# Attention and MLP on one core: four token groups' second layer as seven half-size products, and the attention output kept in a ring

## The chip, the cores and the metric

The kernel runs on one NeuronCore of a Trainium2 chip. The core's engines are TensorE (PE, matrix products into the accumulator memory PSUM), VectorE (DVE), ScalarE (ACT), GpSimd (POOL) and SyncE (SP, which here only issues transfers). Each takes its own instructions in order; semaphores order them among each other. The metric is the device time of one execution in microseconds (us), the median over runs.

## The reference, cut to what matters

The program computes attention with 16 extra "beacon" keys in front of 576 causal ones, for 8 batches and 8 heads of depth 64, and then a two-layer MLP with a gate over all 4608 tokens.

```python
k_all = np.concatenate([beacon_k, k], axis=2)          # 8, 8, 592, 64
scores = scale * np.matmul(q, k_all.transpose(0, 1, 3, 2))
scores = np.where(causal, -1000000000.0, scores)
a = softmax(scores)                                    # over the keys
x = (a @ v_all)  ->  4608 tokens x 512
h = x @ w_in                                           # 512 x 2048
g = h * (1.0 / (1.0 + np.exp(-1.702 * h)))
out = g @ w_out                                        # 2048 x 512, float32
```

## The kernel before, in words

All matrix products have f16 inputs and accumulate in float32.

**Attention.** Work is cut into 16 sets `s`: 8 batches times two half-sets of four heads. For a set, `e_turn` transposes q and k on DVE (line 353), `e_qk` makes scores in chunks of up to 512 columns for four heads (line 382), `e_exp` exponentiates them on ACT (line 393) and `e_mask` clears what is not causal, on POOL (line 414; on DVE for two sets). `e_zadd` adds the exponentials of the key blocks on DVE (line 445: f16, both inputs in SBUF, six additions per set from the fifth set on). `e_av` multiplies by the values (line 467) and `e_norm` writes the normalised result, transposed, to the tile `xT` (line 496), which holds 512 features by all 4608 tokens.

**MLP.** Tokens are taken in ten groups: two of 256 and eight of 512 (`GROUPS`). `e_m1` makes one chunk of the first layer in one PSUM bank: 128 hidden features by 512 tokens as four matmuls of 512 columns (line 518), or, in the groups of 256 tokens, two times 128 features by 256 tokens as eight matmuls of 256 columns. `e_tanh` (ACT, line 532) and `e_gate` (DVE, line 539) turn a chunk into the gated activations, in the group's tile `g` (128 partitions, 16 blocks of hidden features, 512 tokens). A chunk's bank is free again when its gate has read it. `e_m2` is the second layer: for each tile `mt` of 128 tokens it adds up 16 matmuls of 512 columns (line 551), planned in four quarters. `e_evac` copies the result times 0.5 to SBUF on ACT (line 565), `e_store` sends it out from SP (line 571).

**Order.** Nothing is scheduled at run time. The class `Plan` holds every step with an engine, an assumed duration, its dependencies, a priority and a due time, and lays all steps out in one order per engine; the program is emitted in that order. PE steps that need a PSUM bank of the `psu` pool take one of a ring of four (`RING`), the one that is free first. Attention chunks get due times spaced evenly from `T_ATT0` to `T_ATT1`; between them `choose` fills PE with first and second layer steps, in turn if both are ready. The assumed durations only shape the order.

Of the kernel before, what the change touches and what calls it, by code (L numbers as in the profile page):

```python
# [162 lines left out]
def kernel(  # L163
# [37 lines left out]
    ep = ctx.enter_context(tc.tile_pool(name="ep", bufs=NE))  # L201
    zp = ctx.enter_context(tc.tile_pool(name="zp", bufs=2))
    gp = ctx.enter_context(tc.tile_pool(name="gp", bufs=2))
    sp = ctx.enter_context(tc.tile_pool(name="sp", bufs=3))
    pss = ctx.enter_context(tc.tile_pool(name="pss", bufs=1, space=bass.MemoryType.PSUM))
    psu = ctx.enter_context(tc.tile_pool(name="psu", bufs=1, space=bass.MemoryType.PSUM))
# [2 lines left out]
    ones = cst.tile([P, 32], F16, tag="ones", name="ones")  # L209
    w1t = cst.tile([P, NKT, DFF], F16, tag="w1", name="w1")  # L210
    w2t = cst.tile([P, NNT, DMODEL], F16, tag="w2", name="w2")
    xT = cst.tile([P, NKT, NTOK], F16, tag="xT", name="xT")
    bkf = cst.tile([P, NSET, D], F32, tag="bkf", name="bkf")
    bkn = cst.tile([P, 2, D], F16, tag="bkn", name="bkn")
    qn = [cst.tile([P, TR * D], F16, tag=f"qn{i}", name=f"qn{i}") for i in range(NB3)]
# [276 lines left out]

    def e_norm(s, x, half):
        b, hs = divmod(s, HS)
        t0 = b * S + half * HF
        nc.vector.tensor_tensor(  # L496
            out=xT[:, 2 * hs + x, t0 : t0 + HF],
            in0=rings[("av", s, x, half)][:, 0:HF],
            in1=zs[(s, half)][1][:, :],
            op=ALU.mult,  # L500
        )
# [7 lines left out]
    def e_m1(g, n0, n1):  # L509
        t0, t1 = GROUPS[g]  # L510
        w = t1 - t0
        if n0 == 0:
            gts[g] = gp.tile([P, NNT, 512], F16, tag="g", name="g")
        u = ring_tile(("m1", g, n0))
        for nt in range(n0, n1):
            o = (nt - n0) * w
            for kp in range(NKT):
                nc.tensor.matmul(  # L518
                    u[:, o : o + w],
                    w1t[:, kp, nt * P : (nt + 1) * P],  # L520
                    xT[:, kp, t0:t1],
                    start=(kp == 0),
                    stop=(kp == NKT - 1),
                )

    sigs = {}

# [30 lines left out]

    osbs = {}

    def e_evac(g, mt, eng):
        osb = sp.tile([P, DMODEL], F32, tag="osb", name="osb")
        osbs[(g, mt)] = osb
        if eng == "ACT":
            nc.scalar.mul(out=osb[:, :], in_=rings[("m2", g, mt)][:, :], mul=0.5)  # L565
        else:
            nc.vector.tensor_scalar_mul(osb[:, :], rings[("m2", g, mt)][:, :], 0.5)

    def e_store(g, mt):
        t0 = GROUPS[g][0] + mt * P  # L570
        nc.sync.dma_start(out=out[t0 : t0 + P, :], in_=osbs[(g, mt)][:, :])


    T_ATT0, T_ATT1 = 11000, 245000
    NCH0 = 4 * HS
    T_CH = (T_ATT1 - T_ATT0) / (len(CHUNKS) - NCH0)

# [12 lines left out]
        return flight[-1]  # L590

    op = plan.op
    turn, qks, exps, masks, avs, norms = {}, {}, {}, {}, {}, {}
    vload = {}
    gates, m2s = {}, {}
# [83 lines left out]
    def values(s):  # L679
        b, hs = divmod(s, HS)  # L680
        whole = s >= ZSUM
        order = [(2, 1), (2, 0), (0, 0), (1, 0), (0, 1), (1, 1)] if whole else [
            (x, h) for h in range(2) for x in (2, 0, 1)
        ]
        sums, z2 = [], {}
        if whole:
# [16 lines left out]
        for n, (x, half) in enumerate(order):  # L703
            deps = after(s, 0, ETOT) if whole else after(s, half * EHALF, ETOT if half else EHALF)
            if x < 2:
                deps += [vload[(b, j)] for (j, _, _) in AVP[half]] + [vload[(b, -1)]]
# [55 lines left out]
    for j in range(-1, NJ):  # L762
        load_v(1, j)

    def mlp(g):
        t0, t1 = GROUPS[g]
# [7 lines left out]
        old = [m2s[(g - 2, mt, 3)] for mt in range((GROUPS[g - 2][1] - GROUPS[g - 2][0]) // P)] if g > 1 else []  # L774
        n = 512 // w
        for n0 in range(0, NNT, n):
            n1 = n0 + n
            key = ("m1", g, n0)
            pe = op(
                "PE", 4 * n * (w / 2.4 + 2.5), xs + w1_of[n0] + old, lambda n0=n0, n1=n1: e_m1(g, n0, n1),  # L780
                kind="m1", pr=g, ring=key, mode="m", name=f"m1.{g}.{n0}",
            )
            a = op("ACT", 555, [pe], lambda n0=n0, n1=n1: e_tanh(g, n0, n1), pr=1, name="tanh")
            gates[(g, n0)] = op(
                "DVE", 610, [a], lambda n0=n0, n1=n1: e_gate(g, n0, n1), pr=2, closes=key, name="gate"
            )
        for mt in range(w // P):
# [9 lines left out]
            ev = op("ACT", 560, [prev], lambda g=g, mt=mt: e_evac(g, mt, "ACT"), pr=1, closes=key, name="evac")  # L797
            op("SP", 60, [ev], lambda g=g, mt=mt: e_store(g, mt), name="store")

    g = 0  # L800
    for i, ch in enumerate(CHUNKS):
# [11 lines left out]
        for s, c0, c1 in ch:  # L813
            if c1 == ETOT:
                values(s)
                while s % HS == HS - 1 and g < NG and GROUPS[g][1] <= (s // HS + 1) * S:
                    mlp(g)
                    g += 1
    order = plan.run()
    for o in order:  # L820
        o.emit()
# [29 lines left out]
```

## Time and profile before

| | us |
|---|---|
| median of 3 runs | 344.96 (344.85 to 344.98) |
| the profiled execution | 345.13 |
| its span, first to last instruction | 343.4 |
| PE busy in it | 324.2 (94%) |
| DVE busy | 234.3 (68%) |
| ACT busy | 203.6 (59%) |
| POOL busy | 117.2 (34%) |

The granted TensorE clock is full in every one of the page's 40 slices. Line 551, the second layer, has 576 matmuls of 512 columns, 142.5 us busy in the page's list of groups; line 518, the first layer, has 512 of 512 columns and 128 of 256. A matmul's listed duration (379 ns for 512 columns) overlaps with the next one's, so its price in a stream is the spacing of starts. In the timeline attention's last additions over keys run at 248 us, and from then on only the last values and MLP work are left; the last first-layer chunk starts at 324.92 us.

### The profile page before, as it was taken

The numbers are of one execution on the slowest core, as the hardware profiler recorded it, in microseconds if no ns is written. First come the engines' busy times: TensorE is split into PE (matmuls) and PEld (weight loads), VectorE is DVE, ScalarE is ACT, GpSimd is POOL, SyncE is SP. The second block draws the span as 40 slices with busy tenths as digits, with TensorE's granted clock in tenths as the row PEclk, the third lists the DMA queues.
The fourth block names the chain that finished last, engine by engine and source line by source line (L and its number), as shares of the span: only waits on it lengthen the run. The fifth ranks groups of instructions, "written<-read, shape, count | busy, mean of one in ns | idle before, by whom it ended". The sixth has DMA issues, their size and how long they took to land.

```text
span 343.4 us, 9569 instructions
## 1 busy us (share of the span) xinstructions
PE 324.2 (94%) x4104; PEld 172.7 (50%) x4104; DVE 234.3 (68%) x454; ACT 203.6 (59%) x247; POOL 117.2 (34%) x190
## 2 busy tenths in 40 slices
PE   0699899999999999999999999999999999999995
PEld 0476666544554554555454545555444544444442
DVE  3856878499968798998888987987546444444400
ACT  1575587788547775776777676676643444444411
POOL 8765583394256329212653182231100000000000
PEclk9999999999999999999999999999999999999999
DMA  7999999694339149805093396000000000100021
GB/s 128 170 205 209 190 209 110 133 69 74 48 116 142 33 71 87 118 32 103 5 161 64 79 92 111 32 33 34 31 31 32 32 31 31 62 32 31 32 82 71
DMA packets 54122, 28.80 MB, mean 84 GB/s; under 512 B 41280, under 2 KB 45376, under 8 KB 54080
## 3 DMA queue, kind: packets, MB, share of 16 engines
q0 software_dynamic: 47552, 18.49, 46.0%
q1 hardware_dynamic: 6464, 9.69, 7.9%
q8 instruction: 32, 0.52, 0.6%
q14 instruction: 10, 0.08, 0.1%
q10 hardware_dynamic: 64, 0.01, 0.0%
HBM read 37.22 MB, written 9.44 MB: 136 GB/s over the span
## 4 chain that ended last, share of the span: by engine, by line
PE 75%; DVE 11%; issue 5%; POOL 3%; ACT 3%; DMA 2%; SPq 1%; DVEq 0%; POOLq 0%; ACTq 0%
PE u L551 33%; PE u L518 28%; PE u L467 7%; PE s L382 7%; ACT E L393 3%; DVE g L539 3%; DVE zs L445 2%; POOL E L414 2%; DMA bkf<-in_beacon_k_dram 2%; DVE qT L353 1%; DVE kT L353 1%; POOL vb L313 1%; DVE rz L487 1%; DVE zt L478 1%; DVE xT L496 1%
## 5 line engine op out<-in xcount | busy, mean ns | idle before, releaser
L518 PE MATMUL u<-xT,w 128*128 128x512 f16 (+1 forms) x640 | 145.7, 360 | 2.4 <-DVE g L539 1.1
L551 PE MATMUL u<-w,g 128*128 128x512 f16 x576 | 142.5, 379 | 0.0
L539 DVE SCALAR_TENSOR_TENSOR g<-sig,u 128x512 f16<-128x512 f16 x144 | 96.6, 681 | 64.0 <-ACT sig L532 63.2
L532 ACT ACTIVATE sig<-u 128x512 f16<-128x512 f32 x144 | 85.2, 598 | 86.5 <-PE u L518 84.0
L393 ACT ACTIVATE E<-s 128x2048 f16<-128x2048 f32 (+4 forms) x66 | 98.8, 1515 | 26.0 <-PE s L382 25.2
L414 POOL TENSOR_SCALAR_AFFINE_SELECT E<-E 128x512 f16<-128x512 f16 (+3 forms) x90 | 52.8, 612 | 118.3 <-ACT E L393 107.3
L518 PEld LDWEIGHTS <-w 128*128 128x128 f16 x640 | 60.7, 98 | 62.1 <-issue 2.9
L551 PEld LDWEIGHTS <-g 128*128 128x128 f16 x576 | 54.5, 98 | 63.4 <-issue 0.2
L382 PE MATMUL s<-qT,kT 32*128 32x32 f16 (+9 forms) x1544 | 36.0, 227 | 12.2 <-DVE qT L353 10.9
L382 PEld LDWEIGHTS <-kT 32*128 32x128 f16 x1544 | 28.5, 95 | 33.8 <-issue 21.4
L565 ACT ACTIVATE osb<-u 128x512 f32<-128x512 f32 x36 | 21.5, 597 | 22.3 <-PE u L551 22.3
L445 DVE TENSOR_TENSOR zs<-zs,E 128x192 f16<-128x192 f16 (+3 forms) x48 | 27.0, 563 | 4.6 <-ACT E L393 2.7
L467 PE MATMUL u<-E,vb 128*32 128x288 f16 (+4 forms) x1024 | 29.2, 258 | 0.8 <-DVE g L539 0.4
L496 DVE TENSOR_TENSOR xT<-u,rz 128x288 f16<-128x288 f32 x64 | 26.2, 448 | 4.1 <-PE u L467 3.7
L313 POOL DMA_DIRECT2D vb<-in_v_dram x32 | 27.2, 863 | 2.1 <-DMA qn<-in_q_dram 1.4
L467 PEld LDWEIGHTS <-vb 128*32 128x32 f16 (+1 forms) x1024 | 22.6, 98 | 4.6 <-issue 1.9
L353 DVE STREAM_TRANSPOSE kT<-kn 128x576 f32<-128x576 f32 x16 | 20.1, 1257 | 3.8 <-DMA kn<-in_k_dram 2.8
L353 DVE STREAM_TRANSPOSE qT<-qn 128x576 f32<-128x576 f32 x16 | 20.0, 1247 | 0.5 <-DMA qn<-in_q_dram 0.5
L445 DVE TENSOR_TENSOR zs<-E 128x704 f16<-128x704 f16 (+1 forms) x24 | 16.1, 671 | 5.4 <-POOL E L414 3.4
L478 DVE STREAM_TRANSPOSE zt<-u 128x288 f32<-128x288 f32 x32 | 14.0, 463 | 5.6 <-PE u L467 5.6
L487 DVE STREAM_TRANSPOSE rz<-rc 128x288 f32<-128x288 f32 x32 | 15.3, 478 | 1.1
L297 POOL DMA_DIRECT2D kn<-in_k_dram x16 | 9.1, 569 | 2.8 <-DVE g L539 2.0
(27 smaller groups left out, 66.8 us busy)
## 6 DMA issues: line engine op xcount, KB each, us to landing
out_dram<-osb SPq DMA_DIRECT2D x36, 256.0 KB, 2.0
kn<-in_k_dram POOLq DMA_DIRECT2D x16, 288.0 KB, 6.7
qn<-in_q_dram POOLq DMA_DIRECT2D x16, 288.0 KB, 6.3
vb<-in_v_dram POOLq DMA_DIRECT2D x24, 128.0 KB, 5.9
w<-in_moe_w_in_dram POOLq DMA_DIRECT2D x8, 256.0 KB, 9.0
w<-in_moe_w_out_dram POOLq DMA_DIRECT2D x4, 512.0 KB, 13.9
vb<-in_v_dram POOLq DMA_DIRECT2D x8, 112.0 KB, 3.3
vb<-in_v_dram POOLq DMA_DIRECT2D x8, 80.0 KB, 5.3
```

Source lines behind the costliest of these rows:

```text
L313: nc.gpsimd.dma_start(out=t[0 : hi - lo, j, h0:h1, :], in_=v[b, h0:h1, lo:hi, :].rearrange("h n d -> n h d"),)
L353: nc.vector.transpose(out=f32(dst.rearrange("p n e -> p (n e)")).rearrange("p (r t) -> p t r", t=TR), in_=f32(src[:, :]).rearrange("p (t c ...
L382: nc.tensor.matmul(sc[:, h, o : o + w], kT[s % NB2][r : r + 32, j * P : (j + 1) * P, d], qT[s % NB2][r : r + 32, a : a + w, d], start=(d = ...
L393: nc.scalar.activation(out=Es[s][:, :, c0:c1], in_=ss[i][:, :, o : o + c1 - c0], func=AFT.Exp, scale=0.125,)
L414: nc.gpsimd.affine_select(out=blk, in_=blk, compare_op=ALU.is_ge, fill=0.0, base=off + (Nb if j == 0 else 0), pattern=[[0, Q], [1, w]], ch ...
L445: nc.vector.tensor_tensor(out=t[:, :, o : o + w], in0=x, in1=y, op=ALU.add)
L467: nc.tensor.matmul(u[32 * h : 32 * h + 32, a:e], lhs, src[0:kw, h, col : col + e - a], start=first, stop=last,)
L496: nc.vector.tensor_tensor(out=xT[:, 2 * hs + x, t0 : t0 + HF], in0=rings[("av", s, x, half)][:, 0:HF], in1=zs[(s, half)][1][:, :], op=ALU. ...
L518: nc.tensor.matmul(u[:, o : o + w], w1t[:, kp, nt * P : (nt + 1) * P], xT[:, kp, t0:t1], start=(kp == 0), stop=(kp == NKT - 1),)
L532: nc.scalar.activation(out=sig[:, 0:w], in_=rings[("m1", g, n0)][:, 0:w], func=AFT.Tanh, scale=0.851)
L539: nc.vector.scalar_tensor_tensor(out=gts[g][:, n0:n1, 0:w], in0=sigs[(g, n0)][:, 0 : n * w].rearrange("p (n w) -> p n w", n=n), scalar=1.0 ...
L551: nc.tensor.matmul(o[:, :], gts[g][:, nt, mt * P : (mt + 1) * P], w2t[:, nt, :], start=(nt == 0), stop=(nt == NNT - 1),)
```

## The change

For groups 5 to 8 (`NPL` to `NPE`) the second layer, 512 tokens x 2048 x 512, is seen as a product of 2 x 2 quarters: 256 tokens by 1024 features times 1024 features by 256 columns. Strassen's scheme, in Winograd's form, needs seven products of quarters and no eighth; the inputs and outputs are combined by additions.

- Weight sums: `weights` plans four operations on POOL (`e_t`), due from 150 us on, each over 128 x 2048 f16 elements. Three go to new tiles `tB`, the fourth over the tile `bkf`, once all beacon keys have been read from it.
- Activation sums: `products` plans four operations per group on POOL (`e_s`; DVE from group `SDVE` on, which none reaches), each over 128 x 2048 f16 elements, in the order S1, S2, S4, S3. Each of the first three needs the one before it. S1 needs all 16 gates of the group and all products of the previous group, as the tiles `sA` exist once.
- Products: `e_prod` makes one quarter product in one bank as 16 matmuls of 256 columns, each with its own weights (8 feature blocks times two token tiles). Products 1 and 2 need gates alone; 6 needs S2; 5 needs S1; 7 needs S3; 3 needs S4; 4 needs gates and a weight sum.
- Joins: product 1 is copied times 0.5 by ACT (`e_half`); the other six products are added up by seven DVE operations (`e_join`, one input in PSUM, one float32 in SBUF). Product 4's bank is released when its result has been added to the joins of 1, 6 and 7; product 5's is read by two joins.
- Stores: `e_store4` sends a quarter of 256 tokens by 256 columns, 256 KB, from SP; the number of stores per group stays four.
- Ring: `xT` holds 4 x 576 = 2304 tokens. Token t lies at t modulo 2304, and a step of `e_av` whose result will overwrite tokens waits for the first-layer chunks that read them. Group 5 (tokens 2048 to 2560) crosses the end of the ring, so its chunks are two runs of four matmuls of 256 columns.
- The order in which the chunks of groups 5 to 8 are listed follows `SQ`, which at 8 leaves it as it was. `T_ATT0` and `T_ATT1` go from 11 and 245 us to 13 and 235; the assumed spacing of a first-layer matmul from 2.5 to 2.8 ns above its columns' time. The output tiles get their own pool of four buffers (`os`).

```diff
-    xT = cst.tile([P, NKT, NTOK], F16, tag="xT", name="xT")
+    XR = 4 * S
+    NPL, NPE = 5, 9
+    HM, HN = 256, NNT // 2
+    xT = cst.tile([P, NKT, XR], F16, tag="xT", name="xT")
+    sA = [cst.tile([P, HN, HM], F16, tag=f"sA{i}", name=f"sA{i}") for i in range(3)]
+    tB = [cst.tile([P, HN, HM], F16, tag=f"tB{i}", name=f"tB{i}") for i in range(3)]
...
+            cut = max(t0, t1 // XR * XR)
+            for a, e in ((t0, cut), (cut, t1)):
+                for kp in range(NKT if a < e else 0):
+                    nc.tensor.matmul(
+                        u[:, o + a - t0 : o + e - t0],
+                        w1t[:, kp, nt * P : (nt + 1) * P],
+                        xT[:, kp, a % XR : (e - 1) % XR + 1],
...
+    def e_s(g, i, n0, n1, eng):
+        a11, a12, a21, a22 = (quarter(g, x, y)[:, n0:n1, :] for x in range(2) for y in range(2))
+        s1, s2, s4 = (t[:, n0:n1, :] for t in sA)
+        if i == 0:
+            add(eng, s1, a21, a22, ALU.add)
+        elif i == 1:
+            add(eng, s2, s1, a11, ALU.subtract)
+        elif i == 2:
+            add(eng, s4, a12, s2, ALU.subtract)
+        else:
+            add(eng, a21, a11, a21, ALU.subtract)
...
+        for n in range(n0, n1):
+            for mt in range(2):
+                nc.tensor.matmul(
+                    u[:, HM * mt : HM * (mt + 1)],
+                    lhs[:, n, mt * P : (mt + 1) * P],
+                    rhs[:, n, :],
+                    start=(n == 0 and mt == 0),
+                    stop=(n == HN - 1 and mt == 1),
+                )
...
+        nc.vector.scalar_tensor_tensor(
+            out=osbs[(g, dst)][:, :], in0=rings[("p", g, p)][:, :], scalar=0.5, in1=osbs[(g, src)][:, :],
+            op0=ALU.mult, op1=ALU.add,
+        )
...
-    T_ATT0, T_ATT1 = 11000, 245000
+    T_ATT0, T_ATT1 = 13000, 235000
...
+            prev = [op("POOL", 2300, w2_ld + prev, lambda i=i: e_t(i, "POOL"), pr=1, due=150000, name="t")]
...
+        eng = "POOL" if g < SDVE else "DVE"
...
+                d = 150 + 1.0 * 256 * SQ if eng == "POOL" else 70 + 0.7 * 256 * SQ
+                o = op(eng, d, deps, lambda n0=n0, n1=n1, i=i: e_s(g, i, n0, n1, eng), pr=2, name="s")
...
+        prod(1)
+        half = op("ACT", 560, [last[1]], lambda: e_half(g, 1, "m"), pr=1, closes=("p", g, 1), name="half")
+        prod(2)
+        c11 = join(2, "m", "a", [half])
+        store(c11, "a", 0, 0)
+        prod(6)
+        u2 = join(6, "m", "m", [c11])
+        prod(7)
+        u3 = join(7, "m", "u", [u2])
+        prod(4)
+        c21 = join(4, "u", "b", [u3])
+        store(c21, "b", 1, 0)
+        prod(5)
+        u4 = join(5, "m", "m", [u3], False)
+        c22 = join(5, "u", "u", [c21, u4])
+        store(c22, "u", 1, 1)
+        prod(3)
+        c12 = join(3, "m", "m", [u4])
+        store(c12, "m", 0, 1)
```

More of the change, by code (lines that the diff above doesn't have):

```diff
@@ L203 @@
     gp = ctx.enter_context(tc.tile_pool(name="gp", bufs=2))
+    os = ctx.enter_context(tc.tile_pool(name="os", bufs=4))
     sp = ctx.enter_context(tc.tile_pool(name="sp", bufs=3))
@@ L494, in e_norm @@
         b, hs = divmod(s, HS)
-        t0 = b * S + half * HF
+        t0 = (b * S + half * HF) % XR
         nc.vector.tensor_tensor(
@@ L511, in e_m1 @@
         w = t1 - t0
-        if n0 == 0:
+        if g not in gts:
             gts[g] = gp.tile([P, NNT, 512], F16, tag="g", name="g")
@@ L516, in e_m1 @@
             o = (nt - n0) * w
[L517 to L524, printed above, removed]
+            cut = max(t0, t1 // XR * XR)
[5 more added lines that the diff above has]
+                        xT[:, kp, a % XR : (e - 1) % XR + 1],
+                        start=(kp == 0),
+                        stop=(kp == NKT - 1),
+                    )
     sigs = {}
@@ L559, with e_evac @@
     osbs = {}
-    def e_evac(g, mt, eng):
-        osb = sp.tile([P, DMODEL], F32, tag="osb", name="osb")
+    def e_evac(g, mt):
+        osb = os.tile([P, DMODEL], F32, tag="osb", name="osb")
         osbs[(g, mt)] = osb
[L564 to L567, printed above, removed]
+        nc.scalar.mul(out=osb[:, :], in_=rings[("m2", g, mt)][:, :], mul=0.5)
     def e_store(g, mt):
@@ L571, in e_store, with add, tb, e_t @@
         nc.sync.dma_start(out=out[t0 : t0 + P, :], in_=osbs[(g, mt)][:, :])
-    T_ATT0, T_ATT1 = 11000, 245000
+    def add(eng, out, a, b, op):
+        (nc.vector if eng == "DVE" else nc.gpsimd).tensor_tensor(out=out, in0=a, in1=b, op=op)
+    def tb(i):
+        if i < 3:
+            return tB[i][:, :, :]
+        return bkf[:, :, :].bitcast(F16).rearrange("p s e -> p (s e)").rearrange("p (n w) -> p n w", w=HM)
+    def e_t(i, eng):
+        b11, b12 = w2t[:, 0:HN, 0:HM], w2t[:, 0:HN, HM:]
+        b21, b22 = w2t[:, HN:, 0:HM], w2t[:, HN:, HM:]
+        t1, t2, t4, t3 = (tb(x) for x in range(4))
+        if i == 0:
+            add(eng, t1, b12, b11, ALU.subtract)
+        elif i == 1:
+            add(eng, t2, b22, t1, ALU.subtract)
+        elif i == 2:
+            add(eng, t4, b21, t2, ALU.subtract)
+        else:
+            add(eng, t3, b22, b12, ALU.subtract)
@@ new lines, in quarter @@
+    def quarter(g, i, j):
+        return gts[g][:, HN * j : HN * (j + 1), HM * i : HM * (i + 1)]
+    def e_s(g, i, n0, n1, eng):
+        a11, a12, a21, a22 = (quarter(g, x, y)[:, n0:n1, :] for x in range(2) for y in range(2))
+        s1, s2, s4 = (t[:, n0:n1, :] for t in sA)
+        if i == 0:
+            add(eng, s1, a21, a22, ALU.add)
+        elif i == 1:
+            add(eng, s2, s1, a11, ALU.subtract)
+        elif i == 2:
+            add(eng, s4, a12, s2, ALU.subtract)
+        else:
+            add(eng, a21, a11, a21, ALU.subtract)
@@ new lines, in e_prod @@
+    def e_prod(g, p, n0, n1):
+        u = ring_tile(("p", g, p))
+        w = lambda i, j: w2t[:, HN * i : HN * (i + 1), HM * j : HM * (j + 1)]
+        lhs, rhs = {
+            1: (quarter(g, 0, 0), w(0, 0)),
+            2: (quarter(g, 0, 1), w(1, 0)),
+            3: (sA[2], w(1, 1)),
+            4: (quarter(g, 1, 1), tb(2)),
+            5: (sA[0], tb(0)),
+            6: (sA[1], tb(1)),
+            7: (quarter(g, 1, 0), tb(3)),
+        }[p]
+        for n in range(n0, n1):
[7 more added lines that the diff above has]
+                )
@@ new lines, in e_half, with e_join @@
+    def e_half(g, p, dst):
+        t = os.tile([P, DMODEL], F32, tag="osb", name="osb")
+        osbs[(g, dst)] = t
+        nc.scalar.mul(out=t[:, :], in_=rings[("p", g, p)][:, :], mul=0.5)
+    def e_join(g, p, src, dst):
+        if (g, dst) not in osbs:
+            osbs[(g, dst)] = os.tile([P, DMODEL], F32, tag="osb", name="osb")
+        nc.vector.scalar_tensor_tensor(
+            out=osbs[(g, dst)][:, :], in0=rings[("p", g, p)][:, :], scalar=0.5, in1=osbs[(g, src)][:, :],
+            op0=ALU.mult, op1=ALU.add,
+        )
@@ L575, with e_store4 @@
+    def e_store4(g, i, r, c):
+        t0 = GROUPS[g][0] + r * HM
+        nc.sync.dma_start(
+            out=out[t0 : t0 + HM, c * HM : (c + 1) * HM].rearrange("(a p) n -> p a n", p=P),
+            in_=osbs[(g, i)][:, :].rearrange("p (a n) -> p a n", a=2),
+        )
+    T_ATT0, T_ATT1 = 13000, 235000
     NCH0 = 4 * HS
@@ L592 @@
     op = plan.op
+    bkc = {}
     turn, qks, exps, masks, avs, norms = {}, {}, {}, {}, {}, {}
@@ L636, in turns @@
         )
+        bkc[s] = cast
         for which in (1, 0):
@@ L685, in values @@
         sums, z2 = [], {}
+        old = [o for g in m1s if GROUPS[g][0] < (b + 1) * S - XR for o in m1s[g]]
         if whole:
@@ L705, in values @@
             if x < 2:
-                deps += [vload[(b, j)] for (j, _, _) in AVP[half]] + [vload[(b, -1)]]
+                deps += [vload[(b, j)] for (j, _, _) in AVP[half]] + [vload[(b, -1)]] + old
                 deps += [z2[h] for h in range(2) if whole]
@@ L763, with weights, products, prod @@
         load_v(1, j)
+    m1s, done = {}, {}
+    SQ, SDVE = 8, 10
+    def weights():
+        prev = []
+        for i in range(4):
+            prev = [op("POOL", 2300, w2_ld + prev, lambda i=i: e_t(i, "POOL"), pr=1, due=150000, name="t")]
+            tds[i] = prev[0]
+    tds = {}
+    def products(g):
+        eng = "POOL" if g < SDVE else "DVE"
+        sd = {}
+        for n0 in range(0, HN, SQ):
+            n1 = n0 + SQ
+            prev = []
+            for i in range(4):
+                deps = prev + done.get(g - 1, [])
+                for n in range(n0, n1):
+                    deps += [gates[(g, n)], gates[(g, n + HN)]]
+                d = 150 + 1.0 * 256 * SQ if eng == "POOL" else 70 + 0.7 * 256 * SQ
+                o = op(eng, d, deps, lambda n0=n0, n1=n1, i=i: e_s(g, i, n0, n1, eng), pr=2, name="s")
+                prev = [o]
+                sd[(i, n0)] = o
+        lhs = {1: None, 2: None, 3: 2, 4: None, 5: 0, 6: 1, 7: 3}
+        rhs = {1: None, 2: None, 3: None, 4: 2, 5: 0, 6: 1, 7: 3}
+        last = {}
+        def prod(p):
+            prev = []
+            for n0 in range(0, HN, SQ):
+                deps = list(prev)
+                if lhs[p] is not None:
+                    deps.append(sd[(lhs[p], n0)])
+                else:
+                    deps += [gates[(g, n + (HN if p in (2, 4) else 0))] for n in range(n0, n0 + SQ)]
+                if rhs[p] is not None:
+                    deps.append(tds[rhs[p]])
+                o = op(
+                    "PE", 2 * SQ * 109, deps, lambda n0=n0: e_prod(g, p, n0, n0 + SQ), kind="m2", pr=g,
+                    ring=("p", g, p), mode="m", name=f"m2.{g}.{p}.{n0}",
+                )
+                prev = [o]
+            last[p] = prev[0]
+            done.setdefault(g, []).append(prev[0])
+        def join(p, src, dst, deps=(), closes=True):
+            return op(
+                "DVE", 620, [last[p]] + list(deps), lambda: e_join(g, p, src, dst), pr=2,
+                closes=("p", g, p) if closes else None, name="join",
+            )
+        def store(o, i, r, c):
+            op("SP", 60, [o], lambda: e_store4(g, i, r, c), name="store")
+        prod(1)
[17 more added lines that the diff above has]
+        store(c12, "m", 0, 1)
@@ L765, in mlp @@
     def mlp(g):
+        if g == NPL:
+            weights()
         t0, t1 = GROUPS[g]
@@ L773, in mlp @@
                     xs.append(norms[(HS * b + hs, x, half)])
-        old = [m2s[(g - 2, mt, 3)] for mt in range((GROUPS[g - 2][1] - GROUPS[g - 2][0]) // P)] if g > 1 else []
+        old = done.get(g - 2, [])
         n = 512 // w
-        for n0 in range(0, NNT, n):
+        firsts = list(range(0, NNT, n))
+        if NPL <= g < NPE:
+            firsts.sort(key=lambda n: (n % HN // SQ, n))
+        for n0 in firsts:
             n1 = n0 + n
@@ L779, in mlp @@
             pe = op(
-                "PE", 4 * n * (w / 2.4 + 2.5), xs + w1_of[n0] + old, lambda n0=n0, n1=n1: e_m1(g, n0, n1),
+                "PE", 4 * n * (w / 2.4 + 2.8), xs + w1_of[n0] + old, lambda n0=n0, n1=n1: e_m1(g, n0, n1),
                 kind="m1", pr=g, ring=key, mode="m", name=f"m1.{g}.{n0}",
@@ L786, in mlp @@
             )
+            m1s.setdefault(g, []).append(pe)
+        if NPL <= g < NPE:
+            products(g)
+            return
         for mt in range(w // P):
@@ L796, in mlp @@
                 m2s[(g, mt, qt)] = prev
-            ev = op("ACT", 560, [prev], lambda g=g, mt=mt: e_evac(g, mt, "ACT"), pr=1, closes=key, name="evac")
+            done.setdefault(g, []).append(prev)
+            ev = op("ACT", 560, [prev], lambda g=g, mt=mt: e_evac(g, mt), pr=1, closes=key, name="evac")
             op("SP", 60, [ev], lambda g=g, mt=mt: e_store(g, mt), name="store")
@@ L818 @@
                     g += 1
+    for o in bkc.values() if tds else ():
+        tds[3].deps.append(o)
+        tds[3].left += 1
+        o.users.append(tds[3])
     order = plan.run()
```

## The prediction

> **What bounds the kernel now.** I read the page's busy times first, then its chain, then the stretches from 240 us on. TensorE (PE) is busy for 324.2 of the 343.4 us, and the two MLP lines, 518 and 551, hold 61% of the chain that ends last.
>
> ```profile
> PE 324.2 (94%) x4104; PEld 172.7 (50%) x4104; DVE 234.3 (68%) x454; ACT 203.6 (59%) x247; POOL 117.2 (34%) x190
> ...
> PE 75%; DVE 11%; issue 5%; POOL 3%; ACT 3%; DMA 2%; SPq 1%; DVEq 0%; POOLq 0%; ACTq 0%
> ```
>
> The table by stretches (columns: span, then busy us and instructions of PE, PEld, DVE, ACT, POOL, then clock, DMA share, GB/s) says the same of the stage where most of the change lands. PE has no gap, the clock is full, DVE is half idle and POOL has nothing to do.
>
> ```profile
> 240.00:280.00 40.00, 40.00 (x285) 18.82 (x284) 20.35 (x37) 18.48 (x29) 1.49 (x3) 1.00 0.09 34
> 280.00:320.00 40.00, 40.00 (x187) 18.13 (x186) 16.11 (x24) 17.32 (x29) 0.00 (x0) 1.00 0.10 36
> ```
>
> So a microsecond of matmul taken out is a microsecond gained, as long as no new wait on PE takes its place.
>
> **Prices of matmuls**, from the timeline (start, length of the run, count). A run's length holds the whole of its last matmul, so the spacing comes from starts: four of 512 columns start every 0.86 us (264.52 to 265.38), 215.8 ns each; eight of 256 columns take 1.05 us, of which the last is 282 ns (mean of that form), so (1.05 - 0.28) / 7 = 110 ns each, with a weight load before every one of them, as in the products.
>
> ```profile
> 264.52 1.03 PE L551 MATMUL u<-w,g 128*128 128x512 f16 x4
> 265.38 1.03 PE L518 MATMUL u<-xT,w 128*128 128x512 f16 x4
> ...
> 42.01 1.05 PE L518 MATMUL u<-xT,w 128*128 128x256 f16 x8
> ```
>
> **Part 1, the products (groups 5 to 8).** Out: 64 matmuls x 215.8 ns = 13.81 us a group. In: 7 x 16 = 112 matmuls x 110 ns = 12.32 us. Four groups: 4 x 1.49 = **-6.0 us**, all on the path.
>
> **Part 2, the first layer of group 5** is cut at token 2304: 128 matmuls of 256 columns for 64 of 512: 14.08 - 13.81 = **+0.3 us**.
>
> **Part 3, joins, stores, ring of tokens.** A group loses four evacuations on ACT (597 ns) and gains one half-copy there and seven joins on DVE. A gate, the nearest row, occupies DVE for 0.6 us (681 ns, overlapping), so 7 x 0.6 = 4.2 us per group, hidden by the half-idle DVE above. But the products share the four PSUM banks: those of products 4 and 5 stay closed until product 7 is joined, and two banks alternate between first-layer chunks and products. A chunk holds its bank for 2.4 us (below), a chunk and a product take 0.86 + 1.76 = 2.6 us: 0.2 us of slack. I charge **+0.3 us** for the four groups (0 to 1.5). The xT ring lets attention overwrite tokens only after the first layer has read them; the new dependence is of PE on earlier PE work, in order anyway: 0. The stores leave SP in the same number, 2.0 us to landing: 0. POOL's loads of q and k that queue behind the new operations were planned 22 us ahead: 0.
>
> **Part 4, the end.** Before, the last gate is hidden by 64 second-layer matmuls. After, three of the four quarters of the last group's first token tile run early, so the order of instructions has the last first-layer chunk followed by only four second-layer matmuls, each waiting for its own gate.
>
> ```profile
> 324.92 1.03 PE L518 MATMUL u<-xT,w 128*128 128x512 f16 x4
> ...
> 325.99 0.60 ACT L532 ACTIVATE sig<-u 128x512 f16<-128x512 f32 x1 [0.27 <-PE u L518]
> 326.62 0.69 DVE L539 SCALAR_TENSOR_TENSOR g<-sig,u 128x512 f16<-128x512 f16 x1 [1.04 <-ACT sig L532]
> ```
>
> The gate ends at 327.31, 2.39 us after its chunk began and 1.53 us after PE could go on (324.92 + 0.86). Three matmuls fill 0.65: **+0.9 us** (0.6 to 1.6).
>
> **Part 5, the front.** Attention chunks are due from 13 instead of 11 us on and then closer together. PE has some 2 us of gaps between 28 and 66 us now; I charge **+0.6 us** (0 to 1.5).
>
> **Part 6, the sums on POOL: the open price.** Four weight sums and four activation sums per group, each 128 x 2048 in f16 with two inputs. No such POOL operation is in the trace. The nearest rows are the masks, one input, f16:
>
> ```profile
> L414 POOL TENSOR_SCALAR_AFFINE_SELECT E<-E 128x512 f16<-128x512 f16 x30 | 19.8, 658 | 42.6 <-ACT E L393 31.6 <-DVE xT L496 11.0
> ...
> L414 POOL TENSOR_SCALAR_AFFINE_SELECT E<-E 128x192 f16<-128x192 f16 x14 | 5.3, 382 | 0.0
> ```
>
> The slope is (658 - 382) / 320 = 0.86 ns an element; at 2048 elements 0.66 + 1536 x 0.86 = **2.0 us** if a second input is free, and 2.0 + 2048 x 0.86 = **3.75 us** if it costs a pass of its own. I take 2.2 (an estimate), near the first: same engine, type and output; and the planner's constants that rows can check fit them (POOL's issue 560 and 870 against 563 to 569 and 863; gate 610 against 0.6 from start to start), which makes its 2.2 to 2.3 for these sums credible, no more.
>
> What it must not exceed follows from the order of PE's instructions. In groups 6 to 8 the last first-layer chunk of a group is followed by chunk, chunk, product 2, chunk, product 4, chunk, product 6: 4 x 0.86 + 2 x 1.76 = 6.96 us. The sums start with the last gate, 1.6 us in. Product 6 needs two sums in 5.35 us; product 7, two chunks and two products (5.2) later, needs the fourth in 10.6. So up to **2.6 us each they are hidden**; above that PE waits 4x - 10.4 us a group (x in us, 0.2 for the waits between the sums). Group 5 has more PE work between but a weight sum and five masks in POOL's queue too: 5x + 2.5 against 16.3, hidden up to 2.75. At 2.2 all this costs 0.
>
> The Trainium skill speaks against it: "GPSIMD Engine Reference", section 3.1, gives 4.5 us for a two-input add of 2048 fp32 elements on this engine; it has no f16 figure, and no run here shows one. By it the sum would be some 23 us more for groups 6 to 8 and 9 for group 5.
>
> **Part 7, POOL against DVE during attention.** Eight of the sums (four of weights, four of group 5) run while attention's sums over keys (line 445, two SBUF inputs) run on DVE, and the two get in each other's way. A 128x320 mask that lasts 0.47 us elsewhere (159.84) takes 1.06 beside such an addition, and the longest of these additions is 1.22 us where one of 1152 elements takes 0.75 alone (146.44).
>
> ```profile
> 209.04 1.06 POOL L414 TENSOR_SCALAR_AFFINE_SELECT E<-E 128x320 f16<-128x320 f16 x1 [2.84 <-ACT E L393]
> ```
> ```profile
> 209.01 0.76 DVE L445 TENSOR_TENSOR zs<-E 128x1152 f16<-128x1152 f16 x1
> ```
>
> So one waits for the other's whole instruction, now 0.5 us, after the change up to 2.2. Attention starts about one such addition in 2.4 us (6 per set), so a sum of 2.2 us meets 0.9 of them and holds each 1.1 us on average: 8 us of DVE time in all, in a phase where DVE is busy 33 to 37 of 40 us. The 0.5 us waits of now leave almost no gap on PE, so part is absorbed; I charge **+1.5 us** (0 to 8).
>
> **Sum**, against the profiled execution (345.13 us; span 343.4 and 1.7 around it): -6.0 + 0.3 + 0.3 + 0.9 + 0.6 + 1.5 = -2.4, so 342.7; that execution lies 0.17 above the median of 344.96, which gives **342.6 us**. With every cost at its low end -4.8: 340.2.
>
> **Rivals.**
> 1. *The sums on POOL set the pace* (slower). From 2.6 us on, products 6 and 7 wait. At 3.0: 3 x 1.6 + 1.2 = +6, 348.6. At 3.75: 3 x 4.6 + 5 + 1 more for part 7 = +20, **362.5**. Break-even lies at about 2.8 us. For it: two inputs through one engine, and nothing hides a longer chain, as PE's order is fixed. Against it: only the planner's constants. Chance 0.31, of which I leave 0.12 to prices above the upper row.
> 2. *Waits between POOL and DVE eat the gain*: part 7 at 4 to 7 us, **345 to 348**; the gaps on PE would all lie in attention. For: DVE has no reserve there. Against: the present waits, many more of them, cost PE nearly nothing. Chance 0.17 (0.07 within 0.2%, 0.10 slower).
> 3. *Nothing of parts 3 to 7 shows*: near **340.5**. Chance 0.07.
> The forecast, 341.3 to 344.2, keeps 0.45.
>
> Faster than by 0.2% (0.7 us, about what a measurement here tells from no change): 0.45 + 0.07 = 0.52; within: 0.07; slower: 0.31 + 0.10 = 0.41. Forecast alone: 341.3 to 344.2. For 8 in 10 the range must reach to the sums' upper row: 340.4 to 362.5.
>
> **What would show it.** Products at 110 ns spacing and some 318 us of PE work; POOL's sums at about 2.2 us; no idle time of PE before products 6 and 7 that a POOL sum ends; key additions of up to 3 us beside POOL sums; 0.9 us of wait ahead of the last 48 matmuls. A sum above 2.8 us makes the forecast wrong by itself.

## The result, and the profile after

| | before | after |
|---|---|---|
| median, us | 344.9 (344.81 to 344.98, 4 runs) | **383.63** (380.57 to 384.48, 4 runs) |
| the profiled execution, its span | 345.13, 343.4 | 384.1, 382.4 |
| PE busy | 324.2 | 330.0 |
| DVE busy | 234.3 | 275.1 |
| POOL busy | 117.2 | 199.1 |

The ratio after to before is 1.1107 (95% interval 1.1044 to 1.117): 38.7 us slower. The forecast of 342.6 us and the whole range up to 362.5 are missed, on the side of the first rival and beyond it.

The page of the kernel after, in the three lines that answer to those shown of before (busy time by engine; granted clock in 40 slices; the chain that ended last):

```profile
PE 330.0 (86%) x4360; PEld 200.8 (53%) x4360; DVE 275.1 (72%) x482; ACT 195.9 (51%) x235; POOL 199.1 (52%) x210
...
PEclk9999999999999999989999997899999998998999
...
PE 52%; DVE 20%; POOL 14%; DMA 8%; issue 2%; ACT 2%; POOLq 1%; DVEq 0%
```

PE's share of the chain fell from 75% to 52%, and DVE (11% to 20%) and POOL (3% to 14%) took most of its place; DMA's rise from 2% to 8% lies in the loads of the MLP's weights. POOL gained 81.9 us of work for 20 new operations, 4.1 us each. The groups of the kernel after by shape (count, busy us and mean ns, idle before and its releaser) give that price directly:

```profile
L579 POOL TENSOR_TENSOR sA<-g,sA 128x2048 f16<-128x2048 f16 x4 | 16.3, 4064 | 0.2
L579 POOL TENSOR_TENSOR tB<-w 128x2048 f16<-128x2048 f16 x1 | 4.1, 4067 | 0.0
```

A sum with two inputs takes **4.06 us**. The forecast took 2.2, and its upper row was 3.75.

**The place after attention.** What PE waited for from 262 us to the end in the kernel after (total us, times, longest):

```profile
PE u L628 <- POOL sA L579: 7.9, 3, 2.8
PE u L628 <- POOL g L579: 6.6, 3, 2.8
```

These are products 6 (first `tB`, `sA` in order) and 7 of groups 6 to 8: 14.5 us. PE's timeline of the kernel after for group 7 shows what one of them does (start, length, count; in brackets the wait):

```profile
308.31 1.92 PE L628 MATMUL u<-tB,sA 128*128 128x256 f16 x16 [2.80 <-POOL sA L579]
...
316.46 3.48 PE L628 MATMUL u<-bkf,g 128*128 128x256 f16 x16 [2.76 <-POOL g L579]
```

Sixteen matmuls of a product take 1.92 us; behind the second wait the same sixteen take 3.48. The stretches of the kernel after around that place (the last columns: granted clock, DMA share, GB/s) say why:

```profile
308.00:316.00 8.00, 5.39 (x40) 3.83 (x40) 2.07 (x3) 1.19 (x2) 7.92 (x3) 1.00 0.01 2
316.00:320.00 4.00, 3.54 (x17) 2.43 (x18) 0.02 (x1) 0.00 (x0) 0.40 (x1) 0.58 0.00 0
320.00:324.00 4.00, 4.00 (x27) 2.54 (x26) 3.75 (x6) 1.04 (x2) 0.00 (x0) 1.00 0.19 66
```

POOL works without a pause while PE idles; then PE is busy again, but for four microseconds at a granted clock of 0.58. So this wait costs its length and then some 1.7 us more (0.42 x 4). Not every wait does: the product behind the first one, 2.80 us long, ran in 1.92. In each of groups 6 to 8 one of the two waits is followed by such a stretch.

**The place inside attention.** POOL's and then DVE's timeline of the kernel after, in the same stretch:

```profile
151.47 4.07 POOL L579 TENSOR_TENSOR tB<-w 128x2048 f16<-128x2048 f16 x1
...
156.59 4.10 POOL L579 TENSOR_TENSOR tB<-w,tB 128x2048 f16<-128x2048 f16 x1
160.62 0.53 POOL L420 TENSOR_SCALAR_AFFINE_SELECT E<-E 128x320 f16<-128x320 f16 x1
161.12 4.04 POOL L579 TENSOR_TENSOR tB<-w,tB 128x2048 f16<-128x2048 f16 x1
```
```profile
152.25 3.66 DVE L451 TENSOR_TENSOR zs<-E 128x704 f16<-128x704 f16 x1
...
157.17 0.68 DVE L547 SCALAR_TENSOR_TENSOR g<-sig,u 128x512 f16<-128x512 f16 x1
...
158.50 2.32 DVE L451 TENSOR_TENSOR zs<-zs,E 128x192 f16<-128x192 f16 x1
160.74 5.71 DVE L451 TENSOR_TENSOR zs<-E 128x1152 f16<-128x1152 f16 x1
```

Each of the three key additions ends only after a weight sum beside it has ended: 152.25 + 3.66 = 155.91 stands 0.37 us behind 151.47 + 4.07 = 155.54, and the other two stand 0.13 and 1.29 us behind theirs. The third starts before its sum does, but beside the mask of 160.62, and is held through both. Its 1152 elements take 5.71 us; in the kernel before an addition of that shape lasted 0.75:

```profile
146.44 0.75 DVE L445 TENSOR_TENSOR zs<-E 128x1152 f16<-128x1152 f16 x1
```

The gate between them, with one input in PSUM, keeps its 0.68. All key additions together are busy 27.0 + 16.1 = 43.1 us before and 38.8 + 27.3 = 66.1 after (the two groups of the page, first of before, then of after):

```profile
L445 DVE TENSOR_TENSOR zs<-zs,E 128x192 f16<-128x192 f16 (+3 forms) x48 | 27.0, 563 | 4.6 <-ACT E L393 2.7
L445 DVE TENSOR_TENSOR zs<-E 128x704 f16<-128x704 f16 (+1 forms) x24 | 16.1, 671 | 5.4 <-POOL E L414 3.4
```
```profile
L451 DVE TENSOR_TENSOR zs<-zs,E 128x192 f16<-128x192 f16 (+3 forms) x48 | 38.8, 808 | 6.4 <-ACT E L399 3.6
L451 DVE TENSOR_TENSOR zs<-E 128x704 f16<-128x704 f16 (+1 forms) x24 | 27.3, 1137 | 2.3 <-ACT E L399 2.3
```

DVE has no reserve there, so PE waits; its four longest waits in the kernel after from 150 to 262 us:

```profile
PE u L526 <- DVE xT L502: 6.1, 2, 3.1
PE u L473 <- DVE g L547: 5.3, 1, 5.3
PE u L526 <- DVE g L547: 2.5, 1, 2.5
PE u L473 <- DVE zs L451: 2.3, 1, 2.3
```

None names a POOL sum: POOL holds DVE, and DVE's late gates, norms and key additions hold PE, 16.2 us in these four rows.

### The profile page after: what moved, and what is told of

Read it like the earlier page. It is cut to its first block, busy times and chain, and to the rows that moved or that the text cites. A ratio compares the mean times of both kernels' runs of the same rounds, so it can differ in the third digit from the quotient of the medians.

```text
span 382.4 us, 10142 instructions
## 1 busy us (share of the span) xinstructions
PE 330.0 (86%) x4360; PEld 200.8 (53%) x4360; DVE 275.1 (72%) x482; ACT 195.9 (51%) x235; POOL 199.1 (52%) x210
## 4 chain that ended last, share of the span: by engine, by line
PE 52%; DVE 20%; POOL 14%; DMA 8%; issue 2%; ACT 2%; POOLq 1%; DVEq 0%
PE u L526 22%; PE u L559 15%; POOL sA L579 8%; DVE zs L451 8%; PE u L628 6%; PE s L388 5%; PE u L473 5%; DVE g L547 4%; DMA w<-in_moe_w_in_dram 4%; DMA w<-in_moe_w_out_dram 4%; POOL g L579 3%; DVE rz L493 1%; DVE xT L502 1%; DVE zt L484 1%; POOLq L1021 1%
## 5 line engine op out<-in xcount | busy, mean ns | idle before, releaser
L526 PEld LDWEIGHTS <-w 128*128 128x128 f16 x704 | 67.4, 99 | 64.0 <-issue 12.9
L559 PE MATMUL u<-w,g 128*128 128x512 f16 x320 | 79.9, 380 | 1.0 <-DVE g L547 0.5
L559 PEld LDWEIGHTS <-g 128*128 128x128 f16 x320 | 29.8, 98 | 33.9 <-issue 1.4
L388 PE MATMUL s<-qT,kT 32*128 32x32 f16 (+9 forms) x1544 | 36.1, 226 | 12.4 <-DVE qT L359 11.4
L451 DVE TENSOR_TENSOR zs<-zs,E 128x192 f16<-128x192 f16 (+3 forms) x48 | 38.8, 808 | 6.4 <-ACT E L399 3.6
L579 POOL TENSOR_TENSOR sA<-g 128x2048 f16<-128x2048 f16 x4 | 16.7, 4174 | 42.3 <-DVE g L547 42.3
L473 PE MATMUL u<-E,vb 128*32 128x288 f16 (+4 forms) x1024 | 30.6, 261 | 7.2 <-DVE g L547 6.4
L644 DVE SCALAR_TENSOR_TENSOR osb<-u,osb 128x512 f32<-128x512 f32 x28 | 18.8, 685 | 22.6 <-PE u L628 22.5
L628 PEld LDWEIGHTS <-g 128*128 128x128 f16 x256 | 26.7, 105 | 15.8 <-POOL g L579 8.1
L451 DVE TENSOR_TENSOR zs<-E 128x704 f16<-128x704 f16 (+1 forms) x24 | 27.3, 1137 | 2.3 <-ACT E L399 2.3
L628 PEld LDWEIGHTS <-sA 128*128 128x128 f16 x192 | 18.9, 100 | 14.3 <-POOL sA L579 9.4
L628 PE MATMUL u<-tB,sA 128*128 128x256 f16 x128 | 16.2, 282 | 7.9 <-POOL sA L579 7.9
```

Source lines behind the costliest of these rows:

```text
L388: nc.tensor.matmul(sc[:, h, o : o + w], kT[s % NB2][r : r + 32, j * P : (j + 1) * P, d], qT[s % NB2][r : r + 32, a : a + w, d], start=(d = ...
L451: nc.vector.tensor_tensor(out=t[:, :, o : o + w], in0=x, in1=y, op=ALU.add)
L473: nc.tensor.matmul(u[32 * h : 32 * h + 32, a:e], lhs, src[0:kw, h, col : col + e - a], start=first, stop=last,)
L526: nc.tensor.matmul(u[:, o + a - t0 : o + e - t0], w1t[:, kp, nt * P : (nt + 1) * P], xT[:, kp, a % XR : (e - 1) % XR + 1], start=(kp == 0) ...
L559: nc.tensor.matmul(o[:, :], gts[g][:, nt, mt * P : (mt + 1) * P], w2t[:, nt, :], start=(nt == 0), stop=(nt == NNT - 1),)
L579: (nc.vector if eng == "DVE" else nc.gpsimd).tensor_tensor(out=out, in0=a, in1=b, op=op)
```

## The experiments

Theory A: the price of the sums, twice over, makes the loss (PE waits for the sums of groups 6 to 8; inside attention the sums hold DVE). Rival: ring, cut first layer, new due times or the products themselves make it. Later theories concern the few microseconds left once the sums are cheap. "Old pace" is `T_ATT0`, `T_ATT1` and the 2.5 ns of before. Every kernel below is the one after with the edit shown; each ratio is to the kernel before, run alongside at 344.95 to 345.06 us.

### 1. Without the products

```diff
-    NPL, NPE = 5, 9
+    NPL, NPE = 99, 99
```

> No product by quarters at all: every group's second layer as before, no sums on POOL; the ring of 2304 tokens, the cut of group 5's first layer and the attention times of 13 and 235 us stay. Theory A (the POOL sums, at 4.05 us each, are the whole loss, by the waits of products for them and by the key additions on DVE that they hold up): 344 to 347 us, near the kernel before. Rival R (ring, pacing or the cut add waits of their own): over 350 us.

Measured: 347.93 us, ratio 1.0093 (1.0069 to 1.0117). Ring, cut and pace cost 2.9 of the 38.7 us, so these three parts of the rival are out as the main cause; the products themselves are left to experiment 3. The time lies 0.9 above theory A's interval, and 2.9 is more than parts 2 and 5 had (0.9).

### 2. Activation sums of groups 6 to 8 on DVE

```diff
-    SQ, SDVE = 8, 10
+    SQ, SDVE = 8, 6
...
-                d = 150 + 1.0 * 256 * SQ if eng == "POOL" else 70 + 0.7 * 256 * SQ
+                d = 150 + 1.0 * 256 * SQ if eng == "POOL" else 1250
```

> The activation sums of groups 6, 7 and 8 on DVE (planned at 1.25 us); the weight sums and those of group 5 stay on POOL. Theory A: the 14.5 us in which PE waits for POOL sums in groups 6 to 8 go, and some 5 us of slow clock after them, so 362 to 366 us, with the waits between 150 and 240 us unchanged. Rival R2 (the products themselves are the loss: banks, joins): above 375 us.

Measured: 364.3, ratio 1.0555 (1.054 to 1.0571), as theory A says. So 383.63 - 364.3 = **19.3 us** came from these sums: 14.5 are the waits, and the other 4.8 agree with the slow stretches behind them (1.8, 1.7 and 1.7 us, worked out below). The four waits inside attention stand unchanged (6.1, 5.2, 2.5, 2.3).

### 3. All sums on DVE

```diff
-            prev = [op("POOL", 2300, w2_ld + prev, lambda i=i: e_t(i, "POOL"), pr=1, due=150000, name="t")]
+            prev = [op("DVE", 1250, w2_ld + prev, lambda i=i: e_t(i, "DVE"), pr=2, due=100000, name="t")]
...
-    SQ, SDVE = 8, 10
+    SQ, SDVE = 8, 0
```

(with the price of 1250 of experiment 2)

> All weight and activation sums on DVE, planned at 1.25 us each, the weight sums due from 100 us on; POOL has only masks and loads, as before the change. Theory A: no sum can hold a key addition up or keep a product waiting for long, so 341 to 346 us. Rival R2: above 360 us, since the products, banks and joins are all there.

Measured: 346.47, ratio 1.003 (1.0013 to 1.0046), 0.5 above the interval expected. The weight sums and group 5's sums on POOL had cost 364.3 - 346.47 = **17.8 us**. All products, banks and joins are in this kernel, so they are not the main cause either. The group of the same sums in this kernel:

```profile
L579 DVE TENSOR_TENSOR sA<-g,sA 128x2048 f16<-128x2048 f16 x4 | 4.9, 1221 | 0.0
```

1.22 us on DVE against 4.06 on POOL. But even so the kernel is 1.4 us slower than before, where -6 of products should show.

### 4. One input instead of two

```diff
     def add(eng, out, a, b, op):
-        (nc.vector if eng == "DVE" else nc.gpsimd).tensor_tensor(out=out, in0=a, in1=b, op=op)
+        nc.gpsimd.tensor_copy(out=out, in_=a)
```

> Every sum on POOL is replaced by a copy of its first input, same sizes, same tiles written, same order of every engine as the changed kernel (the second input is left out, so the output of groups 5 to 8 is another). Theory A: a copy costs 1.8 to 2.1 us by the slope of the masks (0.86 ns an element), under the 2.6 us that PE's order hides, so no product waits, and key additions are held for 2 us instead of 4: 342 to 348 us. Rival R2: above 370 us. It also tests the forecast's own figure for a price of about 2 us, 342.6 us.

Measured: 346.43, ratio 1.0044 (1.0026 to 1.0061): inside what was expected. This is the plainest test of the cause, as no assumed duration changed and the planned order of every engine is that of the kernel after: 383.63 - 346.43 = 37.2 of the 38.7 us go with the second input. In the profiles 37.7 us go, 27.8 of them idle time of PE and 9.9 PE's busy time (330.0 against 320.1). The copies by shape:

```profile
L579 POOL COPY sA<-g 128x2048 f16<-128x2048 f16 x8 | 15.1, 1891 | 42.8 <-DVE g L547 42.8
```

A copy takes 1.89 us, and no product waits for POOL any more, as the forecast's slack of 2.6 us has it. The second input costs 2.17 us on top of 1.89. And this is nearly the forecast's own price (2.2), yet the time is 346.4, not 342.6. So part of the forecast fails apart from the price.

### 5. Without the products, old pace

```diff
-    T_ATT0, T_ATT1 = 13000, 235000
+    T_ATT0, T_ATT1 = 11000, 245000
...
-                "PE", 4 * n * (w / 2.4 + 2.8), xs + w1_of[n0] + old, lambda n0=n0, n1=n1: e_m1(g, n0, n1),
+                "PE", 4 * n * (w / 2.4 + 2.5), xs + w1_of[n0] + old, lambda n0=n0, n1=n1: e_m1(g, n0, n1),
```

(and the edit of experiment 1)

> As the run without products, but attention due from 11 to 245 us and the first layer priced as before: what is left of the change is the ring of 2304 tokens and the cut of group 5's first layer. Theory P (the 2.9 us that the run without products still loses come from the attention times, which leave PE 3 us of gaps between 40 and 120 us): 345.0 to 345.7 us, the cut's 0.3 us. Theory Q (they come from the ring, whose waits hold attention back): 347 to 348 us, as without this edit.

Measured: 345.05, ratio 1.0003 (0.9994 to 1.0012). The pace alone costs 2.9 in that order, ring and cut 0.1. Two stretches, first of experiment 1 (new pace), then of this kernel (old pace):

```profile
40.00:80.00 40.00, 38.45 (x668) 22.95 (x666) 32.81 (x65) 31.33 (x34) 23.92 (x39) 1.00 1.19 139
80.00:120.00 40.00, 37.39 (x590) 19.95 (x592) 34.79 (x69) 26.53 (x31) 17.79 (x29) 1.00 0.48 67
```
```profile
40.00:80.00 40.00, 39.35 (x680) 23.04 (x679) 30.27 (x58) 32.51 (x35) 25.30 (x42) 1.00 1.16 136
80.00:120.00 40.00, 39.62 (x611) 21.20 (x610) 34.17 (x71) 26.96 (x31) 17.09 (x26) 1.00 0.53 77
```

The gaps of the new pace lie at 40 to 120 us, not at 28 to 66 where part 5 looked: PE is busy 3.1 us less there.

### 6 and 7. Sums on DVE, old pace, products only after attention

Experiment 6 is experiment 3 with the old pace and

```diff
-    NPL, NPE = 5, 9
+    NPL, NPE = 6, 9
```

Experiment 7 has `NPE = 10` besides, so that the last group has products too.

> All sums on DVE, products for groups 6 to 8 only, attention times and first-layer price as before the change. Theory A with P: three groups take 4.5 us off PE, the cut gives back 0.3, the end 0.5 to 0.9, and joins and sums on DVE little more, so 341 to 342.5 us, faster than the kernel before. If the products or their banks cost PE something of their own: 344 us or more.

> As the run with products for groups 6 to 8, and also for the last group, 9: another 1.5 us off PE, but at the end the sums (1.22 us each on DVE), the joins and the stores of the last group have no other work beside them. If these cost under 1.5 us together: 339.5 to 341.5 us; if more: 342 to 344 us.

Measured: 342.2, ratio 0.9925 (0.9912 to 0.9938), and **341.42**, ratio 0.9897 (0.9883 to 0.991), both as expected. The idea of the change works. Page and a stretch after attention of experiment 7:

```profile
PE 319.0 (94%) x4360; PEld 197.5 (58%) x4360; DVE 273.2 (81%) x502; ACT 196.2 (58%) x235; POOL 118.1 (35%) x190
```
```profile
240.00:280.00 40.00, 40.00 (x385) 26.73 (x374) 35.29 (x55) 15.71 (x24) 2.47 (x3) 1.00 0.10 34
```

PE has 5.2 us less work than before (319.0 against 324.2), no gap in that stretch and the full clock; DVE carries the sums in the half that the table of before showed idle. It is the fastest kernel of the study, 1.0% under the one before: 3.5 of part 1's 6.0 us arrive.

### 8. The planner told the true price

```diff
-            prev = [op("POOL", 2300, w2_ld + prev, lambda i=i: e_t(i, "POOL"), pr=1, due=150000, name="t")]
+            prev = [op("POOL", 4070, w2_ld + prev, lambda i=i: e_t(i, "POOL"), pr=1, due=150000, name="t")]
...
-                d = 150 + 1.0 * 256 * SQ if eng == "POOL" else 70 + 0.7 * 256 * SQ
+                d = 4070 if eng == "POOL" else 70 + 0.7 * 256 * SQ
```

> The changed kernel with all sums on POOL, but planned at 4.07 us each, so that PE's order puts more work ahead of the products that need them. Theory A: the waits of products 6 and 7 on POOL shrink from 14.5 us, but the weight sums and those of group 5 still hold key additions up for up to 5 us at a time during attention, so 365 to 375 us. If only the planner's wrong price is the cause: 345 to 355 us.

Measured: 383.83, ratio 1.1108 (1.1063 to 1.1152): both expectations missed. PE's waits in the whole of this kernel:

```profile
PE s L388 <- DVE qT L359: 11.3, 3, 8.7
PE u L628 <- DVE g L547: 7.4, 8, 1.4
PE u L526 <- DVE g L547: 5.2, 4, 2.5
PE u L473 <- DVE g L547: 5.0, 6, 2.2
```

The first row is the wait at the start, 11.4 us in the kernel after too. No row of the whole list names a POOL sum: the planner moved other work ahead of products 6 and 7. In place of those 14.5 us the products wait for gates (7.4 us, against 0.2 in the kernel after), PE's other waits after the start grow by 3.9 us in all, and PE is busy 333.3 us against 330.0. Part of that is the hold inside attention, which a planner that takes the engines for independent doesn't see; how much is due to the four banks, of which products 4 and 5 keep two, the rows don't separate.

### 9. One input, old pace

Edits of experiments 4 and 5 (products on).

> The run with copies in place of the sums on POOL (the second input is left out, so the output of groups 5 to 8 is another), with attention times and first-layer price as before the change. It is the forecast's own case, a price near 2 us with the front's loss taken out. The forecast's sum without part 5 says 345.0 - 6.0 + 0.3 + 0.3 + 0.9 + 1.5 = 342.0; theory P says 346.4 less the 2.9 us that the attention times cost, 343.5; if parts 3 and 7 are far larger than charged, over 345 us.

Measured: 346.3, ratio 1.0042 (1.0028 to 1.0056): the third case; the pace gives nothing back here. The 2.9 us of experiment 5 don't add to the rest: PE's gaps move from the stretch of 40 to 120 us to that of 120 to 280 us.

### 10. Only the sums of groups 6 to 8 on POOL

Experiment 3, with the weight sums on DVE due from 140000, and

```diff
-        eng = "POOL" if g < SDVE else "DVE"
+        eng = "DVE" if g < 6 else "POOL"
```

> The converse of the run with the sums of groups 6 to 8 on DVE: here the weight sums (due from 140 us) and group 5's sums are on DVE and those of groups 6 to 8 on POOL, planned at their wrong price. Theory A, with the two losses separate: the run with everything on DVE, 346.5, plus the 19.3 us that groups 6 to 8 cost on POOL: 364 to 368 us, with no key addition held for more than 1.3 us. If the waits on DVE during attention had been what cost the later groups too: under 355 us.

Measured: 363.59, ratio 1.0537 (1.0522 to 1.0551). Just under the times expected, and 17.1 above experiment 3. So from the other side the sums of groups 6 to 8 cost 17.1 us where experiment 2 had 19.3; the planner lays out an order of its own in each, so the two losses are known to about 2 us. One addition of the last set did stand beside group 6's first sum and lasted 3.86 us, against the expectation. Two lines of PE's timeline in this kernel:

```profile
264.86 3.41 PE L628 MATMUL u<-bkf,g 128*128 128x256 f16 x16 [1.78 <-POOL g L579]
...
291.17 2.99 PE L628 MATMUL u<-tB,sA 128*128 128x256 f16 x16 [2.79 <-POOL sA L579]
```

Here a first wait of 2.79 us is followed by slow matmuls (2.99 us); in the kernel after the one at 308.31, 2.80 long, was not. And the wait at 264.86, only 1.78 long, is followed by a product of 3.41 us.

### 11 and 12. What holds back the forecast at a low price

Experiment 11 is experiment 9 with `NPL = 6` (copies on POOL, no products in attention); experiment 12 is experiment 6 with `NPL = 5` (sums on DVE, group 5's products in attention).

> As the last run with copies in place of the sums on POOL (second input left out) and the old attention times, but products for groups 6 to 8 only. What that run lost, 346.3 us, came between 120 and 280 us. Theory G (group 5's products, its sums and its banks, run inside attention, where DVE frees the banks late): without them 341.5 to 342.7 us, like the run with all sums on DVE for the same groups (342.2). Theory H (2 us operations on POOL beside attention's key additions are the loss, the four weight copies included): 344 us or more.

> All sums on DVE, old attention times, products for groups 5 to 8: the run of 342.2 us with group 5 added. Theory G: group 5's products inside attention cost more than the 1.5 us that they take off PE, with POOL quite out of it: 343.5 to 346 us. Theory H: 340.5 to 341.5 us.

Measured: 345.28, ratio 1.0011 (1.0 to 1.0022), and 344.37, ratio 0.9982 (0.9973 to 0.9991). The first speaks for POOL's operations in attention as the cause, the second for group 5's products; both count. With sums on DVE, group 5's products cost 344.37 - 342.2 = 2.2 (although they take 1.5 of matmuls away); with products in groups 6 to 8 alone, copies on POOL in place of sums on DVE cost 345.28 - 342.2 = 3.1. Measured against the other partner (experiment 9), the two are 346.3 - 345.28 = 1.0 and 346.3 - 344.37 = 1.9. Every pair has an order of its own from the planner, so the exact shares stay open.

## Why the prediction was wrong, step by step

The 38.7 us divide so: 19.3 from the sums of groups 6 to 8 on POOL (experiment 2), 17.8 from the weight sums and group 5's (experiment 3), and 1.6 that remain against before with every sum on DVE. As experiment 10 shows, the split between the first two holds to about 2 us.

**Part 6, the price of a sum, is the step that failed.** "I take 2.2" against 4.06 measured. The upper bound of 3.75, a second pass at the masks' slope, was too low as well: the second input costs 2.17 us where a whole copy takes 1.89 (experiment 4). The choice near the lower end rested on the planner's constants. They had fitted gates and issues, and said nothing of an operation that no row showed.

The Trainium skill's 4.5 us ("GPSIMD Engine Reference", section 3.1, fp32 at 2048 elements), which the prediction weighed and set aside for its type, is much nearer than the 2.2 taken: the f16 sum of this case takes 4.06, between the prediction's upper row and that figure.

The order of events in part 6 held for groups 6 to 8. The formula 4x - 10.4 gives 5.84 us a group at 4.06; groups 7 and 8 waited 5.56 and 5.55, group 6, with the last of attention's work in between, 3.40. Below 2.6 nothing was to wait, and nothing did at 1.89. For group 5 it did not hold: 5x + 2.5 - 16.3 is 6.5 us at 4.06, and none of its products waited for a sum; DVE held PE up beside them. With the price right and everything else as written the prediction would have said 342.6 + 17.5 + 6.5 + 1 = 367.6 (groups 6 to 8, group 5, and rival 1's addition for part 7), so the price set too low is the largest fault but not the whole of it.

**Part 7 had the right mechanism at too small a size.** One engine waits for the other's whole instruction, and the trace of before had shown it with 0.5 us masks. With sums of 4.06 us the additions grow by 66.1 - 43.1 = 23 us, 2.9 for each of eight sums, and PE waits 16.2 us in the four rows above (2.5 in the same stretch of experiment 4, at 1.89 us). The prediction charged 1.5 (0 to 8), and its first rival only "1 more" at a high price. The hope that part would be absorbed came from stops of 0.5 us; it doesn't carry to stops of 4. At 1.89 us the same item measures 1.9 to 3.1 (experiment 11 against 6, and 9 against 12), above the 1.5 but inside its bounds.

**Not priced at all: the clock after a wait.** Behind some of PE's waits stand stretches of some four microseconds whose mean granted clock is 0.54 to 0.87. Worked out from how much longer the same runs of matmuls last there, they cost about 9 us in all: 1.3 at 167 to 170 us, 2.8 near 236 to 242, 1.8 at 274 to 280, 1.7 each at 316 and 350. The 9.9 us by which PE is busier than in experiment 4, with the same order of work, say the same. Rival 1 at 3.75 us (362.5) left them out too.

**Part 1 was right.** Sixteen matmuls of a product in 1.91 us are (1.91 - 0.28) / 15 = 109 ns each, against 110. **Part 2 was right** in size: ring and cut together cost 0.1 (experiment 5) for 0.3.

**Part 3 was half right.** After attention neither banks nor joins cost PE a gap from 240 to 320 us in experiments 6 and 7. Inside attention group 5's products and joins cost a net 1.0 to 2.2 us, which the step, reading DVE's slack from 240 us on for all four groups, did not see.

**Part 4 was right.** In the kernel after:

```profile
366.46 1.10 PE L559 MATMUL u<-w,g 128*128 128x512 f16 x3
368.04 2.33 PE L559 MATMUL u<-w,g 128*128 128x512 f16 x10 [0.47 <-DVE g L547]
```

Three matmuls, 0.65 us of work, are followed 1.58 us after their start by the next: 0.93 us of wait, against 0.9.

**Part 5 was too small.** 2.9 us by experiments 1 and 5, outside its bounds of 0 to 1.5, and in another place than the one read. It depends on the order: with the products in, the old pace gives almost nothing back (experiment 9 against 4).

**Two slips in the sum.** With every cost at the low end that its part states, the sum is -6.0 + 0.3 + 0.6 = -5.1 and the time 339.9 us, not 340.2; and rival 3, with nothing of parts 3 to 7, stands at 339.3, not 340.5. Neither bears on the result.

So the forecast of a gain had two faults. At the measured price the first rival's mechanism decides. But even at the price assumed, the kernel would not have been faster: with copies of 1.89 us it takes 346.4. In attention group 5's products (part 3) and POOL's operations (part 7) cost more than they were charged (experiments 11 and 12), and so does part 5 when it stands alone. These costs can't simply be added, so how they share the 3.8 us between 346.4 and the forecast stays open. The gain is there to be had where DVE has room: sums on DVE and products only after attention give 341.42.

## What to carry to other kernels

An operation whose form no row shows should be priced with a full pass of its own for every input, and the forecast should go by that until a run says otherwise (here that price, 3.75 us, was still under the 4.06 measured); the assumed durations in a scheduler are no measurement. A two-input operation on POOL beside two-input operations on DVE is priced by the longer of the two instructions, and by who waits for DVE, not by POOL's idle time. Before a saving is counted on one stage's slack, each place where the change lands should be read by itself: the same products gained after attention and lost inside it.

## What the runs showed of the hardware

- A POOL operation of 128 x 2048 f16 elements takes 1.89 us with one input and 4.06 with two; DVE does the latter in 1.22 us.
- A DVE addition with both inputs in SBUF and a two-input POOL operation exclude each other for whole instructions: additions of 0.5 to 0.75 us became 3.66 and, behind a mask and a sum in a row, 5.71. A DVE operation with one input in PSUM isn't held (0.68 us beside the same sum).
- The Trainium skill states this exclusion ("SBUF — State Buffer", section "Who interferes with whom"), and these traces agree with it (5.71 us with two inputs in SBUF, 0.68 with one).
- A PE wait of 1.4 to 2.8 us can be followed by about four microseconds at a lower granted clock (0.58 at 316 us), and need not be: of two waits of 2.8 us, the one at 308.31 in the kernel after left the clock at 1.00, the one at 291.17 in experiment 10 was followed by a product of 2.99 us in place of 1.92. Of two waits of 1.41 us in experiment 8, the one at 321.50 left it at 1.00, and behind the one at 350.65 it was 0.60 for four microseconds; other waits of 0.5 to 1.4 us stand ahead of both. What decides it these runs do not show.
- The Trainium skill ("TensorE: Matmul & The Clock Gate", Part 1) speaks of free-running windows of about 3.4 us, after an idle one of which the clock falls to half. That the same wait falls now on one side, now on the other would agree with a free-running window; that 2.33 us at 274.40 in the kernel after, and 1.78 us in experiment 10, were enough does not agree with a whole idle one.
